# A fifth polynomial tile in every second unit of an attention kernel's first branch

## The chip, the cores and the metric

One core of a Trainium2 chip runs the whole program. The metric is the device time of one execution in microseconds (us).

The five engines work side by side, each through a list of instructions in a fixed order: PE (matrix products; PEld is its weight load), ACT (here nearly only exponentials), DVE and POOL (elementwise work), and SP, which issues most transfers. An instruction that must wait for another engine holds up everything behind it in its own list.

## The reference

Two attention blocks, both over 2048 rows of 1024 columns with 32 heads of 32 columns, all in bf16; the outputs stand side by side.

```
# branch A: full softmax attention
qkv = x @ wqkv
p = softmax(q @ k^T * 32**-0.5)          # 2048 x 2048 in each of 32 heads
a = (p @ v) @ wo

# branch B: four segments of 512 rows; causal softmax inside a segment,
# and a linear memory of the segments before
p = softmax(q_s @ k_s^T * 32**-0.5 + mask)
o = g * (phi(q_s) @ M) / (phi(q_s) @ z + 1e-6) + (1 - g) * (p @ v_s)
M += phi(k_s)^T @ v_s;  z += sum(phi(k_s))     # phi(t) = t + 1 if t > 0 else exp(t)
b = o @ wo

out = concatenate([a, b], axis=-1)
```

## The kernel before

**Units, sets and tiles.** Branch A is cut into 64 units (g, c): four heads (group g, 0 to 7) and 256 queries (c, 0 to 7). A unit has 8 sets of 4 tiles, one tile for each head of the group: 128 partitions by 512 columns, that is two blocks of 128 keys against 256 queries. Branch B has 16 units of 5 such sets, two groups of heads of one segment in each; they are spread among the units of A. The first four units of A are cut into parts, and their sets follow the loading of the input.

**The way of a set.** PE makes the scores (`plan_set`, the products of L1208) in four of six PSUM banks, which serve as three slots of two. ACT turns a slot at a time into `P` (`plan_exp`, L1303: 128 x 1024 elements, scale, exp and a conversion to bf16 in one instruction). Then PE multiplies `P` by the values (L1416) and by ones (L1423) for the sums (`round`); DVE and POOL divide and transpose (`turned`, L1530 to L1550). The two other banks, 6 and 7, take these sums and the projections (the products of L847), whose results DVE copies out (L1623). The text `BANKS` gives the bank of each in turn.

**Polynomial tiles.** Some tiles of A skip ACT. Of a marked set, head 0's tile is computed as a parabola that stands for the exponential of a small argument: DVE reads the scores from PSUM, scales and shifts them into `Y` (L1251, `plan_cube`), POOL squares `Y` into `Z` (L1260) and makes `Pc` of it (L1261, `parabola`). ACT's first exp of that set then has 512 columns instead of 1024. `Y` and `Pc` have three buffers each and `Z` two; the same buffers of `Y` and `Z` serve `phi` of branch B (L1922, `job_phi`), which ends in the same two POOL instructions. A path with ACT's exp is there for arguments that are too large, behind a flag; these inputs do not need it.

Which sets are marked follows from

```
CUBIC = {"3": (0, 2, 4), "4": (0, 2, 4, 6), "5": (0, 1, 2, 4, 6)}
WHOLE = {("A", 7, 7): (0, 2, 4), ("A", 7, 6): (0, 2, 4, 6)}
    def cubed(self, unit, part):
        if unit[0] != "A" or part is not None:
            return ()
        if unit in WHOLE:
            return WHOLE[unit]
        n = 8 * unit[1] + unit[2] if unit[1] < 6 else 48 + PAIR.index(unit[1:])
        return CUBIC[POLYS[n]]
```

`POLYS` has a digit for each unit of A, all of them 4. `PAIR` is the order of the last 16 units. With the four cut units (no polynomial tile) and the two of `WHOLE` this makes 58 x 4 + 4 + 3 = 239 tiles.

**The order.** A planner lays the sets along ACT's time (in `plan_set`, a set with a polynomial tile is shorter by 512 columns), spreads the projections between their ready and due times (`plan_jobs`, `level`), and a list scheduler (`Prog.schedule`) makes one list of instructions for each engine from estimated durations. `rearrange` then changes these lists by `MOVES`: texts for PE, ACT, DVE and POOL, in which "a+b" goes on by a places and takes the instruction b places later forward to here. The lists are fixed from then on; semaphores hold each instruction until what it reads is there.

Of the kernel before, what the change touches and what calls it, by code (L numbers as in the profile page):

```python
# [25 lines left out]
    "666767676767666767766766676667666766676666676666766676666676767767666667666667676767676666766666766676766776766676666766"  # L26
    "667676677676667666667666766676676666667676677676666676666676667666776766776766676666676667666676766776766667666666767667"
    "767666766666766667666766676666666667677676767666667666766676766676767667676667666666676676677676666676666766666667766776"
    "766667666667666766667666667667667666766767767666677666666667676776766666767666667677676766676666667676776766676667666766"
    "67666676666666676666766"  # L30
# [13 lines left out]
POLYS = "4444444444444444444444444444444444444444444444444444444444444444"  # L44
# [101 lines left out]
class Op:  # L146
# [17 lines left out]
    def __hash__(self):  # L164
# [650 lines left out]
class _Kernel:  # L815
# [339 lines left out]
    def cubed(self, unit, part):  # L1155
# [5 lines left out]
        n = 8 * unit[1] + unit[2] if unit[1] < 6 else 48 + PAIR.index(unit[1:])  # L1161
        return CUBIC[POLYS[n]]

# [1132 lines left out]
```

## Time and profile before

| | |
|---|---|
| median of 3 runs | 1057.99 us (1056.72 to 1060.06) |
| profiled execution | 1057.04 us, of which 1055.3 us from its first to its last instruction (the span) |
| busy: PE, ACT, POOL, DVE | 1025.1, 1001.6, 725.4, 708.0 us |
| TensorE clock granted | 1.000 |
| exps of 1024 and of 512 columns | 939 and 239 |
| polynomial tiles | 239 |

Busy is the time in which at least one instruction of the engine runs. The ends of matrix products are modelled by the profiler, so a busy PE is not a PE at its peak. The chain of work that ended last is followed back from the last instruction: at each step to what released it, or to the instruction before it on its engine. A wait is put down to the releaser that came last. The lines of these views stand in the prediction.

### The profile page before, as it was taken

The page shows a single profiled execution, that of the slowest core. Times are in us where ns is not written, and L with a number is a line of the kernel's source. Part 1 is how long each engine was busy: PE and PEld are TensorE (multiplying, and loading weights), DVE is VectorE, ACT ScalarE, POOL GpSimd, SP SyncE. Part 2 cuts the span into 40 slices and gives each one's busy share as a digit, 9 for nine tenths or more (in the row PEclk, how much of TensorE's full clock was granted, in tenths as well). Part 3 has the DMA queues.
Part 4 walks back from the last instruction along what each step waited for, and adds up shares of the span by engine and source line. Part 5 has one row for each costly group of instructions (what it writes and reads, how often), then busy time and mean ns, then how long its engine had stood idle before and what let it go on. Part 6 is the DMA issues. An engine that isn't in the chain of part 4 may idle for free.

```text
span 1055.3 us, 55116 instructions
## 1 busy us (share of the span) xinstructions
PE 1025.1 (97%) x25168; PEld 549.9 (52%) x25168; DVE 708.0 (67%) x1451; ACT 1001.6 (95%) x1193; POOL 725.4 (69%) x999
## 2 busy tenths in 40 slices
PE   8999999999999999999999999999999999999998
PEld 4456555566454455556544454466555545445444
DVE  3446667766656878787647888877556787774444
ACT  4999999999999999999999999999999799999996
POOL 1004677766767888889857897988657688885643
PEclk9999999999999999999999999999999999999999
DMA  9223351007202431034321322033121750022101
GB/s 182 41 43 92 69 140 24 18 14 151 66 28 80 118 85 19 5 59 101 94 73 41 84 57 47 17 86 81 34 77 43 212 147 4 28 78 78 33 23 58
DMA packets 171802, 71.99 MB, mean 68 GB/s; under 512 B 135472, under 2 KB 169776, under 8 KB 171568
## 3 DMA queue, kind: packets, MB, share of 16 engines
q1 hardware_dynamic: 169200, 67.67, 26.7%
q8 instruction: 198, 3.24, 1.3%
q10 hardware_dynamic: 2368, 0.79, 0.3%
q14 instruction: 36, 0.29, 0.1%
HBM read 45.23 MB, written 11.67 MB: 54 GB/s over the span
## 4 chain that ended last, share of the span: by engine, by line
PE 66%; ACT 24%; DVE 5%; POOL 2%; issue 1%; SPq 1%; DMA 0%; ACTq 0%; DVEq 0%; POOLq 0%
PE ps L847 32%; ACT P L1303 24%; PE ps L1208 13%; PE ps L1416 10%; PE ps L1423 9%; DVE Y L1251 1%; DVE T L1530 1%; SPq L1587 1%; POOL Z L1260 1%; PE ps L1877 1%; PE ps L1653 1%; ACT P L1281 1%; DMA xT_A<-in_A_x_dram 0%; DVE OT_B L1959 0%; DVE KQ_B L1623 0%
## 5 line engine op out<-in xcount | busy, mean ns | idle before, releaser
L1303 ACT ACTIVATE P<-ps 128x1024 bf16<-128x1024 f32 (+1 forms) x1178 | 991.9, 988 | 31.7 <-PE ps L1208 16.8
L1260 POOL TENSOR_TENSOR Z<-Y 128x512 f32<-128x512 f32 x287 | 305.6, 1068 | 206.3 <-DVE Y L1251 179.1
L1423 PE MATMUL ps<-P,onesb 128*32 128x256 bf16 (+1 forms) x4386 | 301.0, 270 | 0.0
L1416 PE MATMUL ps<-P,V_A 128*32 128x256 bf16 x3618 | 257.2, 274 | 0.1
L1251 DVE TENSOR_SCALAR Y<-ps 128x512 f32<-128x512 f32 x239 | 163.6, 685 | 113.8 <-PE ps L1208 101.1
L1208 PE MATMUL ps<-KQ_A 32*128 32x256 bf16 x4096 | 203.8, 272 | 10.5 <-ACT P L1303 5.4
L1261 POOL TENSOR_SCALAR Pc<-Z 128x512 bf16<-128x512 f32 x239 | 154.5, 650 | 12.0
L1208 PEld LDWEIGHTS ps<-KQ_A 32*128 32x128 bf16 x4096 | 62.5, 92 | 165.9 <-ACT P L1303 113.0
L1423 PEld LDWEIGHTS ps<-P,onesb 128*32 128x32 bf16 x4386 | 128.6, 96 | 31.4 <-issue 16.0
L847 PE MATMUL ps<-xT_B,W_B 128*32 128x512 bf16 (+1 forms) x2200 | 140.7, 366 | 1.3 <-issue 0.2
L847 PE MATMUL ps<-xT_A,W_A 128*32 128x512 bf16 (+1 forms) x2156 | 140.1, 370 | 1.8 <-DMA xT_A<-in_A_x_dram 1.2
L1416 PEld LDWEIGHTS ps<-P,V_A 128*32 128x32 bf16 x3618 | 107.7, 96 | 34.1 <-issue 15.7
L1416 PE MATMUL ps<-Pc,V_A 128*32 128x256 bf16 x478 | 122.2, 273 | 0.0
L1423 PE MATMUL ps<-Pc,onesb 128*32 128x256 bf16 x478 | 122.1, 273 | 0.0
L1332 POOL TENSOR_SCALAR_AFFINE_SELECT P<-P 128x768 bf16<-128x768 bf16 (+1 forms) x96 | 76.1, 802 | 36.3 <-ACT P L1303 35.4
L1530 DVE STREAM_TRANSPOSE T<-ps 128x512 f32<-128x512 f32 x122 | 86.5, 709 | 16.9 <-PE ps L1423 12.5
L847 PEld LDWEIGHTS ps<-xT_B,W_B 128*32 128x32 bf16 x2200 | 52.8, 96 | 47.2 <-issue 21.8
L847 PEld LDWEIGHTS ps<-xT_A,W_A 128*32 128x32 bf16 x2156 | 50.7, 96 | 46.0 <-issue 13.0
L847 PE MATMUL ps<-Wo_B,OT_B 128*32 128x512 bf16 (+1 forms) x1052 | 70.9, 375 | 0.1
L847 PE MATMUL ps<-Wv_B,xT_B 128*32 128x512 bf16 (+1 forms) x1064 | 69.2, 373 | 0.5 <-DVE T L1441 0.4
L1548 POOL TENSOR_TENSOR T<-T,rc 128x256 bf16<-128x256 f32 x74 | 49.1, 664 | 23.1 <-DVE rc L1533 21.7
L1623 DVE CAST outsb<-ps 128x512 bf16<-128x512 f32 x56 | 38.7, 691 | 37.2 <-PE ps L1416 14.8
(107 smaller groups left out, 1197.7 us busy)
## 6 DMA issues: line engine op xcount, KB each, us to landing
Wv_B<-in_B_wv_dram SPq DMA_DIRECT2D x32, 256.0 KB, 3.4
W_B<-in_B_wk_dram SPq DMA_DIRECT2D x32, 256.0 KB, 3.3
W_B<-in_B_wq_dram SPq DMA_DIRECT2D x32, 256.0 KB, 4.3
Wo_B<-in_B_wo_dram SPq DMA_DIRECT2D x32, 256.0 KB, 3.6
out_dram<-outsb SPq DMA_DIRECT2D x56, 128.0 KB, 1.9
W_A<-in_A_wqkv_dram SPq DMA_DIRECT2D x14, 256.0 KB, 3.9
ot_a_scratch<-OTst SPq DMA_DIRECT2D x50, 64.0 KB, 1.9
xT_A<-ot_a_scratch SPq DMA_DIRECT2D x6, 512.0 KB, 4.9
```

The lines of the kernel that those rows point to most:

```text
L847: ins = e.matmul(out[r], w[:, r], x, start=start, stop=stop, tile_position=(0, 32 * t), skip_group_check=True)
L1208: ins = e.matmul(out, kap, qap, start=st, stop=True, tile_position=(32 * h, 0), skip_group_check=True)
L1251: o = self.dve(lambda e: e.tensor_scalar(Y[:, :], src, SCALE, MID, ALU.mult, ALU.add), 512, key - 9.0, [self.bank[bank]], [rY], fixed=0.15)
L1260: self.pool(lambda e: e.tensor_tensor(Z[:, :], Y[:, :], Y[:, :], ALU.mult), 512, key, [rY], [rZ], rate=0.58)
L1261: return self.pool(lambda e: e.tensor_scalar(dst, Z[:, :], C2, REST, ALU.mult, ALU.add), 512, key, [rZ], [rP], rate=TS_RATE)
L1303: a = self.act(guarded if early and not free else lambda e: e.activation(dst, src, ACT.Exp, scale=SCALE), cols, key, rd, wr, fixed=EXP_FIXED)
L1332: self.pool(lambda e: e.affine_select(v, v, pattern=pat, compare_op=ALU.is_ge, fill=0.0, base=0, channel_multiplier=-1), 2 * nd * P, key + ...
L1416: ins = e.matmul(self.ps[32 * h:32 * h + 32, 512 * obk + q0:512 * obk + q0 + nq], v, p, start=first, stop=last, tile_position=(0, 32 * h), ...
L1423: ins = e.matmul(self.ps[32 * h:32 * h + 32, lcol + q0:lcol + q0 + nq], self.onesb[:, 0:32], p, start=False, stop=last, tile_position=(0, ...
L1530: self.dve(lambda e: e.transpose(T2[:, :], src), 512, k - NORM_K, [obk.res], [ro, rl], fixed=0.17)
L1548: self.pool(lambda e: e.tensor_tensor(half.rearrange("p (b r) -> p b r", r=32), ov, bc, ALU.mult), QC, k, [ro, rr], [rl], rate=0.435)
L1623: self.dve(lambda e: e.tensor_copy(dst, src), 512, key, [self.at(b)], rdst, fixed=0.155)
```

## The change

Every second digit of `POLYS` becomes 5, so that these units take a polynomial tile in set 1 too. The planner's lists and the turns of the banks come out differently, so `BANKS` is new, and so are the texts of `MOVES` for PE, ACT, DVE and POOL: 2933 moves instead of 3463 for PE, 30 instead of 50 for ACT, 1229 instead of 1213 for DVE, 772 instead of 836 for POOL, found by a search that began at the planner's own order. No other line differs.

```diff
 BANKS = (
-    "666767676767666767766766676667666766676666676666766676666676767767666667666667676767676666766666766676766776766676666766"
...
+    "666767667767666767766766676667666766676666676666766676666676767676676667666667676677676666766666766676766776766667666766"
...
 )
...
-POLYS = "4444444444444444444444444444444444444444444444444444444444444444"
+POLYS = "4545454545454545454545454545454545454545454545454545454545454545"
 CUBIC = {"3": (0, 2, 4), "4": (0, 2, 4, 6), "5": (0, 1, 2, 4, 6)}
...
 MOVES = {
     "PE": (
-        "39+1 3+1 1+3 3+1 1+2 1+3 1+1 1+1 1+1 2+1 1+1 1+1 1+1 1+1 1+1 1+1 1+1 1+1 1+1 1+1 1+1 1+1 1+1 1+1 1+1 1+1 1+1 1+1 1+7 7+1 "
...
```

More of the change, by code (lines that the diff above doesn't have):

```diff
@@ L25 @@
 BANKS = (
-    "666767676767666767766766676667666766676666676666766676666676767767666667666667676767676666766666766676766776766676666766"
[L27 to L30, printed above, removed]
+    "666767667767666767766766676667666766676666676666766676666676767676676667666667676677676666766666766676766776766667666766"
+    "667676677676667666667666766676666666667676677676666676666676666667676766776766676676676666666676766776766677666666767667"
+    "767666676666766667666766677666666767667676767667667666766666666676767667676677666666676676677676666676666766666667766776"
+    "766667666667666766667666667667666666766767767677667666666677676776766766766666667677676766676666667676776766676667666766"
+    "67666766666666676666767"
 )
@@ L202 @@
     "PE": (
[123 rows of a table removed]
[103 rows of a table added]
     ),
     "ACT": (
-        "6+1 11+1 1+1 1+1 1+1 1+1 1+1 15+1 1+1 1+1 1+1 1+1 1+1 1+1 1+1 1+1 1+1 1+1 1+1 1+1 1+1 1+1 52+1 1+1 1+1 1+1 1+1 1+1 1+1 "
-        "1+1 1+1 1+1 1+1 1+1 1+1 1+1 1+1 1+1 1+1 1+1 1+1 1+1 1+1 1+1 1+1 1+1 1+1 1+1 1+1 1+1 "
+        "6+1 11+1 1+1 1+1 1+1 1+1 1+1 1+1 14+1 1+1 1+1 1+1 1+1 1+1 1+1 1+1 1+1 1+1 1+1 56+1 1+1 1+1 1+1 1+1 1+1 1+1 1+1 1+1 1+1 "
+        "1081+1 "
     ),
     "DVE": (
[41 rows of a table removed]
[42 rows of a table added]
     ),
     "POOL": (
[28 rows of a table removed]
[26 rows of a table added]
     ),
```

362 rows, old and new, of the table MOVES are left out of this document.

## The prediction

> **What bounds the kernel now.** I read the profile's page first, its chain above all, then the groups by line and shape, then busy time in stretches of 25 us, then the waits, and last the chain inside one stretch.
>
> ```profile
> span 1055.3 us, 55116 instructions
> ...
> PE 1025.1 (97%) x25168; PEld 549.9 (52%) x25168; DVE 708.0 (67%) x1451; ACT 1001.6 (95%) x1193; POOL 725.4 (69%) x999
> ...
> PE 66%; ACT 24%; DVE 5%; POOL 2%; issue 1%; SPq 1%; DMA 0%; ACTq 0%; DVEq 0%; POOLq 0%
> PE ps L847 32%; ACT P L1303 24%; PE ps L1208 13%; PE ps L1416 10%; PE ps L1423 9%; DVE Y L1251 1%; DVE T L1530 1%; SPq L1587 1%; POOL Z L1260 1%; PE ps L1877 1%; PE ps L1653 1%; ACT P L1281 1%; DMA xT_A<-in_A_x_dram 0%; DVE OT_B L1959 0%; DVE KQ_B L1623 0%
> ```
>
> Two engines are nearly full: PE has 30.2 us without work, ACT 53.7 us. The chain says which of them an edit has to shorten: two thirds of the span it runs over PE, a quarter over the exps of L1303. So a microsecond taken from ACT is, on average over the span, worth about a quarter of one. POOL holds 2% of the chain.
>
> The two limits alternate. In the next view the columns are the stretch, its length, and the busy time (with instruction counts) of PE, PEld, DVE, ACT and POOL; the second fence is the same view for the masking of branch B's diagonal tiles (L1332) alone, which shows where units of B lie.
>
> ```profile
> 325.00:350.00 25.00, 25.00 (x596) 12.51 (x588) 17.63 (x29) 24.53 (x31) 20.36 (x24) 1.00 0.19 49
> ...
> 575.00:600.00 25.00, 23.21 (x603) 11.66 (x595) 22.84 (x50) 24.89 (x31) 19.43 (x28) 1.00 0.25 67
> 600.00:625.00 25.00, 25.00 (x620) 13.07 (x612) 19.20 (x36) 23.48 (x29) 23.77 (x33) 1.00 0.32 70
> 625.00:650.00 25.00, 23.09 (x568) 11.75 (x560) 23.01 (x52) 22.92 (x28) 19.01 (x27) 1.00 0.17 40
> 650.00:675.00 25.00, 24.77 (x620) 12.90 (x614) 18.95 (x38) 22.33 (x27) 23.39 (x34) 1.00 0.11 25
> ...
> 925.00:950.00 25.00, 24.21 (x570) 11.89 (x562) 18.64 (x36) 24.25 (x29) 20.60 (x32) 1.00 0.24 77
> ...
> sum 1050.00, PE 1024.40 PEld 549.78 DVE 706.69 ACT 1000.97 POOL 725.43; mean PE 24.39 PEld 13.09 DVE 16.83 ACT 23.83 POOL 17.27
> ```
>
> ```profile
> 575.00:600.00 25.00, 4.87 (x6) 1.00 0.25 67
> 600.00:625.00 25.00, 0.00 (x0) 1.00 0.32 70
> ```
>
> At 575 us, with units of B, ACT is full and PE has 1.8 us to spare. At 600 and 650 us, with units of A alone, PE is full and ACT already idles 1.5 and 2.7 us. The polynomial tiles exist in units of A only: the change relieves ACT mainly where PE is the limit. And in the same stretches POOL, which has 31% to spare over the span, has 1.2 and 1.6 us left of 25.
>
> **The change: what moves.** Of the 32 entries that become 5, four do nothing. The first four units of branch A are cut into parts and take no polynomial tile (this drops the entries of units (0,1) and (0,3)), and (7,6) and (7,7) have their own sets in WHOLE. So 28 units gain one tile each, set 1.
>
> ```profile
> L1303 ACT ACTIVATE P<-ps 128x1024 bf16<-128x1024 f32 x939 | 910.7, 1076 | 26.5 <-PE ps L1208 12.0 <-PE ps L1423 9.7 <-DVE Y L1922 1.3
> L1260 POOL TENSOR_TENSOR Z<-Y 128x512 f32<-128x512 f32 x287 | 305.6, 1068 | 206.3 <-DVE Y L1251 179.1 <-DVE bias L1729 5.3 <-DVE bias L1725 3.8
> ...
> L1251 DVE TENSOR_SCALAR Y<-ps 128x512 f32<-128x512 f32 x239 | 163.6, 685 | 113.8 <-PE ps L1208 101.1 <-POOL Z L1260 3.8 <-PE ps L1423 2.3
> L1261 POOL TENSOR_SCALAR Pc<-Z 128x512 bf16<-128x512 f32 x239 | 154.5, 650 | 12.0
> L1303 ACT ACTIVATE P<-ps 128x512 bf16<-128x512 f32 x239 | 154.3, 645 | 5.2 <-PE ps L1208 4.8
> ```
>
> *ACT.* 28 exps go from 1024 to 512 columns. By busy time one saves 910.7/939 - 154.3/239 = 0.970 - 0.645 = 0.325 us; by mean duration 1076 - 645 = 0.431 us. Halving the columns should halve what scales with them, so I take 0.43: 28 x 0.43 = 12.0 us, and 9.1 us as the low end. ACT's count stays at 1193; its busy time goes to about 990. Of the 12.0 us the chain's share is 24%: -2.9 us. The ends: nothing, if every relieved exp lies where PE leads, and -12.0, if the projections of L847 can be pushed into the stretches where PE has room.
>
> *PE.* The matmuls are the same. 56 pairs of groups (28 tiles, two halves, values and sums) read Pc instead of P; no time.
>
> *DVE.* 28 x 0.685 = 19.2 us more, 708 to 727 us, 69% of the span: free as work. But the tile's PSUM bank is now released by DVE, and the next score matmuls on PE wait for that.
>
> ```profile
> PEld ps L1208 <- ACT P L1303: 133.9, 382, 1.0
> ...
> PEld ps L1208 <- issue: 31.9, 122, 0.8
> ...
> ACT P L1303 <- PE ps L1208: 16.8, 34, 3.2
> ...
> PEld ps L1208 <- DVE Y L1251: 16.3, 45, 0.5
> ...
> DVE Y L1251 <- POOL Z L1260: 3.8, 6, 1.0
> ```
>
> Columns: total us, times, longest. Score matmuls that waited for nothing shown ("issue") still have 31.9/122 = 0.26 us before them; with Y as the releaser it is 16.3/45 = 0.36. The excess is 0.10 x 45 = 4.5 us over 239 tiles, 0.5 us over 28; if all 16.3 counts, 1.9 us. I take 1.0, between the two.
>
> *POOL.* 28 x (1.068 + 0.650) = 48.1 us more, 725 to 774 us, 73%. The same view for PEld alone has PE's waits for it:
>
> ```profile
> PEld ps L1416 <- POOL Pc L1261: 0.6, 3, 0.3
> ```
>
> So POOL has been late rarely: PE waited for Pc three times, DVE for a Y buffer (the row above) six times of 287. What happens when it is late shows in one place. This is the chain in the window 870 to 925 us (start, duration, what):
>
> ```profile
> 911.28 0.36 PE ps L1208 x8
> 911.66 0.70 DVE Y L1251
> 912.43 1.05 POOL Z L1260
> 913.56 0.63 POOL Pc L1261
> 914.26 1.10 POOL Z L1260
> 915.45 0.70 DVE Y L1251
> 916.22 1.05 POOL Z L1260
> 917.35 0.63 POOL Pc L1261
> 918.05 1.05 POOL Z L1260
> 919.20 0.69 DVE Y L1251
> 920.04 0.42 PE ps L1208 x8
> 920.48 5.20 ACT P L1303 x6
> ```
>
> The three Y buffers were full, so DVE could not write the next Y at 914 us; it waited for POOL to square an older one, the PSUM bank stayed taken, and the score matmuls and then the exps stood behind it. Some eight microseconds (911.66 to 920.04) went at POOL's pace. Set 1 makes this likelier: tiles come from sets 0, 1 and 2, three in a row, where today every second set brings one. Over 512 sets of A (64 units of 8) and 80 of B, ACT's 1001.6 us make 1.69 us for a set; POOL needs 1.72 us for its two instructions of a tile and has the outputs' products and the masking of B besides. Three in a row fill the Y and Pc rings (3 each) at once, and the Z ring has 2.
>
> Where POOL has half its time free, this is absorbed. Sixteen of the 38 full stretches from 100 us on have POOL at 20 us or more (first and last quoted above, at 325 and 925); the 28 units lie evenly, so 28 x 16/38 = 12 extra tiles fall there. Each costs nothing or 1.72 us of the chain: 0 to 20.6 us. The groups of POOL in the window 870 to 925 us give how many squarings it held:
>
> ```profile
> L1260 POOL TENSOR_TENSOR Z<-Y 128x512 f32<-128x512 f32 x17 | 18.0, 1057 | 4.4 <-DVE Y L1251 3.8
> ```
>
> Four of these 17 stand in the stretch of chain shown, and two more in the rest of that window's chain:
>
> ```profile
> 875.96 1.05 POOL Z L1260
> ...
> 877.78 1.09 POOL Z L1260
> ```
>
> That is 6 of 17, 35%. By the row of waits it is 6 of 287, 2%. I take a third, because the twelve are in windows as full as this one and get the three in a row on top: 12 x 1.72 / 3 = +6.9 us.
>
> *One rule of the skill.* The squares of L1636 on DVE read two operands from SBUF, and their durations spread far:
>
> ```profile
> L1636 DVE TENSOR_TENSOR sqA<-KQ_A x64: 374/424/1260, 11.1 to 831.3; 128x512 bf16<-128x512 bf16 x64
> ```
>
> These 64, and 64 like them for B, meet POOL's added 48.1 us, 4.6% of the span; at 1.260 - 0.374 = 0.89 us a meeting this is 128 x 0.046 x 0.89 = 5.2 us more on DVE, which at 69% has room, so nothing in the sum. The Trainium skill, "SBUF — State Buffer", section "Who interferes with whom", says that such a DVE instruction and a GpSimd one that reads SBUF exclude each other for the whole instruction; the spread agrees, and by that rule the upper end of DVE's part would be 5.2 us higher.
>
> *The order.* BANKS changes, and the lists of moves are new for PE, ACT, DVE and POOL. No row prices an order that has not run. Bounds: if the waits of PE for exps (133.9 us) grow by an eighth, +16 us; if ACT's 16.8 us of waiting for scores shrink by a third, -5.6. I take 0 and keep both for the range. SP's queue keeps its instructions.
>
> **Sum.** -2.9 + 1.0 + 6.9 = +5.0 us. The profiled execution took 1057.04 us (1.7 us around its span), the median of the runs is 1057.99, 0.95 above it; the difference is applied to the median: 1063.0 us. A change of 0.3%, 3.2 us, is about what a measurement of this kernel can tell from none.
>
> **Rivals.**
> *ACT's time is given back (faster).* The chain runs over exps for 24% of the span, and PE has 1.8 us to spare in windows such as 575. If the projections move into those, half to all of the 12.0 us return: -6 to -12, 1046 to 1052 us. For it: ACT is the engine with the most fixed work outside PE. Against: the relieved stretches are those where PE is at 25.00. Chance 0.29.
> *ACT only idles more (no change).* PE leads in A, POOL's lateness hides behind the order of PE, which holds the polynomial tiles' products back: 1055 to 1061 us, 1058 the middle. For it: 0.6 us of PE waits for Pc. Chance 0.25.
> *The forecast, POOL late three in a row (slower).* It decides from the point where POOL's other work in a unit exceeds what is left beside five tiles, about 4.9 us in a unit of 13.5 (8 x 1.69 less 5 x 1.72). Own range 1061.2 to 1070 us. Chance 0.38.
> *The new order is worse as a whole.* +16 us, 1074 us, with PE waits for exps up everywhere, POOL full or not. Chance 0.08.
>
> **How the numbers follow.** Faster by over 0.3%: 0.29. Within: 0.25. Slower: 0.38 + 0.08 = 0.46. The range goes from 1047, near full use of ACT's saving, to 1073, near the bad order; outside are about 0.05 below and 0.06 above, and what I cannot name. Cases of both signs hold most of the chance; the likeliest one's own range stands above.
>
> **What would show it.** ACT busy near 990 us, with 267 exps of 512 columns and 911 of 1024; POOL near 774 us; 267 Pc. Right: more waits of DVE Y for POOL Z than 6, and POOL's share of the chain above 2%, in stretches where POOL was at 20 us or more. Wrong: PE's idle time falls below 30.2 us with POOL's share unchanged (the first rival), or ACT's idle time rises by about 12 us at the same span (the second). If PE's wait for exps grows where POOL has room, it is the order.

## The result, and the profile after

After takes 1060.91 us (median of 20 runs, 1058.89 to 1065.79), before on the same chip 1058.05 (1056.67 to 1060.13): ratio 1.0034, 95% interval 1.0026 to 1.0041, slower by about 3 us. The forecast was 1063.0. Its sign and size held. Its main reason did not: the added work on POOL shows no cost here, and what costs is the new order, which the sum had entered as 0.

Lines of after are numbered 21 lower: L1303 is now L1282, L1208 L1187, L1251 L1230, L1260 L1239, L1261 L1240, L1416 L1395, L847 L826. The page of after: span, busy times, chain.

```profile
span 1060.2 us, 55229 instructions
...
PE 1024.3 (97%) x25136; PEld 551.8 (52%) x25136; DVE 724.1 (68%) x1479; ACT 994.1 (94%) x1193; POOL 772.5 (73%) x1055
...
PE 66%; ACT 22%; DVE 6%; POOL 2%; issue 1%; SPq 1%; DMA 1%; ACTq 0%; DVEq 0%; POOLq 0%
```

POOL has its 47 us more and DVE its 16, and POOL's share of the chain is what it was, 2%. ACT is busy 7.5 us less, but its idle time went from 53.7 to 66.1 us and the span up by 4.9; PE idles 35.9 us instead of 30.2. The groups of after by shape:

```profile
L1282 ACT ACTIVATE P<-ps 128x1024 bf16<-128x1024 f32 x911 | 887.8, 1069 | 33.7 <-PE ps L1187 17.2 <-PE ps L1402 9.5 <-DVE Y L1901 2.1
L1239 POOL TENSOR_TENSOR Z<-Y 128x512 f32<-128x512 f32 x315 | 335.8, 1069 | 183.5 <-DVE Y L1230 155.4 <-DVE rc L1512 5.3 <-DVE bias L1704 3.7
...
L1240 POOL TENSOR_SCALAR Pc<-Z 128x512 bf16<-128x512 f32 x267 | 174.4, 658 | 16.1 <-PE ps L1402 1.8 <-PE ps L1395 1.4 <-PE ps L826 1.1
L1282 ACT ACTIVATE P<-ps 128x512 bf16<-128x512 f32 x267 | 169.6, 635 | 12.2 <-PE ps L1187 8.8 <-PE ps L1402 2.6
```

All counts are as announced. What is new is the idle time ahead of the exps, and that PE's scores end it. The waits of after (total us, times, longest):

```profile
PEld ps L1187 <- ACT P L1282: 123.2, 346, 1.2
...
PEld ps L1187 <- issue: 35.6, 135, 0.6
...
ACT P L1282 <- PE ps L1187: 26.0, 48, 1.7
...
PEld ps L1187 <- DVE Y L1230: 16.3, 45, 0.6
...
DVE Y L1230 <- POOL Z L1239: 2.2, 3, 1.0
PEld ps L1395 <- POOL Pc L1240: 2.1, 8, 0.4
```

DVE waited for a Y buffer three times, before six times; PE's waits for Pc grew by 1.5 us in all. So POOL is hardly later than before. ACT waits more for scores (16.8 before, 26.0 now), and PE less for exps (133.9, now 123.2): the balance has tipped from ACT to PE.

The picture of the three full Y buffers is not gone: after's chain has it once (start, duration, what).

```profile
261.00 0.70 DVE Y L1230
...
261.77 1.05 POOL Z L1239
...
263.72 1.05 POOL Z L1239
264.79 0.70 DVE Y L1230
...
267.62 1.05 POOL Z L1239
...
268.76 0.69 DVE Y L1230
```

These 8.5 us are as long as the prediction's stretch at 911 us in before. `a_none`, in which the 28 added tiles are 8 columns wide, has the same stretch at 262 us, so the added load is not what makes it.

Where in the span? Both kernels run the same 1184 exps in the same order, so the end of the n-th exp, counted from 0, shows where one falls behind the other (us; the column of before is absolute, the others are differences to it; the last four are experiments told below):

| exp | before | after | a_none | mid | out | ends |
|---|---|---|---|---|---|---|
| 224 | 213.1 | -1.5 | -0.4 | 0.0 | -1.7 | -0.8 |
| 448 | 402.8 | +0.2 | +3.2 | +1.1 | +0.6 | +1.6 |
| 512 | 459.1 | -0.8 | +2.5 | +0.1 | +0.6 | +1.7 |
| 560 | 501.7 | +3.6 | +6.9 | +6.8 | +1.8 | +2.6 |
| 816 | 725.1 | +8.1 | +12.3 | +10.0 | +2.2 | +3.2 |
| 896 | 793.5 | +6.0 | +10.8 | +7.6 | +1.8 | +2.9 |
| 1168 | 1031.7 | +5.2 | +11.6 | +7.9 | +2.7 | +3.6 |

After is level up to exp 512 and falls back by 8.9 us between 512 and 816. Not all of that is time lost. These are the busy times between the two exps (columns as in the prediction), before and then after:

```profile
459.13:725.06 265.93, 257.84 (x6696) 142.90 (x6686) 201.28 (x406) 255.15 (x305) 221.53 (x302) 1.00 0.29 66
```

```profile
458.32:733.15 274.83, 262.51 (x6836) 148.47 (x6832) 211.47 (x422) 253.90 (x305) 237.25 (x321) 1.00 0.29 66
```

PE has 4.7 us more to do there: 1.7 that before does ahead of exp 512, and 3.0 that before does behind exp 816. This is work moved, not time lost. The loss is in PE's idle time, 4.2 us more (12.3 instead of 8.1), since its work over the whole span is the same within 0.8 us. Up to the end of an exp that idle time adds up to (us):

| exp | before | after | a_none |
|---|---|---|---|
| 448 | 9.7 | 10.2 | 13.3 |
| 512 | 11.1 | 12.0 | 15.7 |
| 816 | 19.2 | 24.3 | 28.3 |
| 1168 | 25.2 | 31.2 | 36.9 |

Of the 6.0 us that after loses by exp 1168, 4.2 fall between 512 and 816; `a_none` loses some in every stretch.

The steepest part of the first table is exps 512 to 560. There the busy times are, before and then after:

```profile
459.10:501.70 42.60, 41.11 (x1237) 26.89 (x1232) 33.50 (x72) 41.03 (x50) 39.20 (x56) 1.00 0.50 102
```

```profile
458.30:505.20 46.90, 43.90 (x1312) 29.03 (x1308) 38.06 (x77) 41.00 (x50) 41.89 (x60) 1.00 0.46 93
```

ACT does the same 41.0 us of work. After's list places 75 more matmuls in it, PE has 2.8 us more to do and idles 1.5 us more, and the stretch is 4.3 us longer. Its chain by line, before and then after:

```profile
by line: ACT P L1303 44.9%; PE ps L847 26.9%; PE ps L1208 11.2%; PE ps L1416 8.6%; PE ps L1423 7.3%; DVE T L1530 1.7%; issue 1.3%; PE ps L1708 0.1%
```

```profile
by line: PE ps L826 43.0%; PE ps L1395 14.0%; PE ps L1187 12.9%; PE ps L1402 11.8%; DVE T L1509 5.7%; DVE Y L1230 3.0%; DVE V_A L1602 2.7%; DVE PKQ_B L1915 2.2%; issue 1.6%; DVE T L1420 1.5%; DVE KQ_A L1602 1.5%; DVE OT_B L1938 1.4%; DVEq L
```

In before's list exps are the largest item of this chain; in after's they are not on it, the projections lead with 43%, and POOL does not appear.

### The profile page after: what moved, and what is told of

Read it like the earlier page. It is cut to its first block, busy times and chain, and to the rows that moved or that the text cites. A ratio compares the mean times of both kernels' runs of the same rounds, so it can differ in the third digit from the quotient of the medians.

```text
span 1060.2 us, 55229 instructions
## 1 busy us (share of the span) xinstructions
PE 1024.3 (97%) x25136; PEld 551.8 (52%) x25136; DVE 724.1 (68%) x1479; ACT 994.1 (94%) x1193; POOL 772.5 (73%) x1055
## 4 chain that ended last, share of the span: by engine, by line
PE 66%; ACT 22%; DVE 6%; POOL 2%; issue 1%; SPq 1%; DMA 1%; ACTq 0%; DVEq 0%; POOLq 0%
PE ps L826 32%; ACT P L1282 22%; PE ps L1187 13%; PE ps L1395 10%; PE ps L1402 9%; PE ps L1856 1%; SPq L1566 1%; DVE Y L1230 1%; POOL Z L1239 1%; DVE T L1509 1%; DVE KQ_B L1602 1%; DVE PKQ_B L1915 1%; DMA xT_A<-in_A_x_dram 0%; PE ps L1632 0%; POOL Pc L1240 0%
## 5 line engine op out<-in xcount | busy, mean ns | idle before, releaser
L1282 ACT ACTIVATE P<-ps 128x1024 bf16<-128x1024 f32 (+1 forms) x1178 | 984.1, 970 | 45.9 <-PE ps L1187 26.0
L1239 POOL TENSOR_TENSOR Z<-Y 128x512 f32<-128x512 f32 x315 | 335.8, 1069 | 183.5 <-DVE Y L1230 155.4
L1230 DVE TENSOR_SCALAR Y<-ps 128x512 f32<-128x512 f32 x267 | 182.8, 685 | 111.9 <-PE ps L1187 101.2
L1395 PE MATMUL ps<-P,V_A 128*32 128x256 bf16 x3562 | 256.7, 274 | 1.0 <-DVE T L1509 0.5
L1187 PE MATMUL ps<-KQ_A 32*128 32x256 bf16 x4096 | 204.4, 272 | 12.2 <-ACT P L1282 7.1
L1240 POOL TENSOR_SCALAR Pc<-Z 128x512 bf16<-128x512 f32 x267 | 174.4, 658 | 16.1 <-PE ps L1402 1.8
L1187 PEld LDWEIGHTS ps<-KQ_A 32*128 32x128 bf16 x4096 | 62.7, 92 | 165.5 <-ACT P L1282 105.8
L1402 PEld LDWEIGHTS ps<-P,onesb 128*32 128x32 bf16 x4330 | 128.6, 96 | 26.8 <-issue 12.4
L826 PE MATMUL ps<-xT_A,W_A 128*32 128x512 bf16 (+1 forms) x2160 | 140.2, 370 | 1.7 <-DMA xT_A<-in_A_x_dram 1.0
L826 PE MATMUL ps<-xT_B,W_B 128*32 128x512 bf16 (+1 forms) x2160 | 139.6, 370 | 1.5 <-DVE cols L1695 0.2
L1395 PE MATMUL ps<-Pc,V_A 128*32 128x256 bf16 x534 | 136.5, 274 | 0.7 <-POOL Pc L1240 0.2
L1402 PE MATMUL ps<-Pc,onesb 128*32 128x256 bf16 x534 | 135.7, 273 | 0.0
L1395 PEld LDWEIGHTS ps<-P,V_A 128*32 128x32 bf16 x3562 | 107.5, 96 | 28.6 <-issue 12.2
L826 PEld LDWEIGHTS ps<-xT_B,W_B 128*32 128x32 bf16 x2160 | 51.5, 96 | 46.1 <-issue 21.4
L826 PEld LDWEIGHTS ps<-xT_A,W_A 128*32 128x32 bf16 x2160 | 50.4, 96 | 45.9 <-issue 14.6
L826 PE MATMUL ps<-Wo_B,OT_B 128*32 128x512 bf16 (+1 forms) x1052 | 71.2, 375 | 0.0
L826 PE MATMUL ps<-Wv_B,xT_B 128*32 128x512 bf16 (+1 forms) x1076 | 69.2, 370 | 0.3 <-DVE rc L1512 0.2
L1395 PEld LDWEIGHTS ps<-Pc,V_A 128*32 128x32 bf16 x534 | 51.3, 96 | 27.7 <-issue 12.7
L1602 DVE CAST KQ_A<-ps 128x512 bf16<-128x512 f32 x60 | 41.3, 689 | 34.7 <-PE ps L826 33.8
```

The lines of the kernel that those rows point to most:

```text
L826: ins = e.matmul(out[r], w[:, r], x, start=start, stop=stop, tile_position=(0, 32 * t), skip_group_check=True)
L1187: ins = e.matmul(out, kap, qap, start=st, stop=True, tile_position=(32 * h, 0), skip_group_check=True)
L1230: o = self.dve(lambda e: e.tensor_scalar(Y[:, :], src, SCALE, MID, ALU.mult, ALU.add), 512, key - 9.0, [self.bank[bank]], [rY], fixed=0.15)
L1239: self.pool(lambda e: e.tensor_tensor(Z[:, :], Y[:, :], Y[:, :], ALU.mult), 512, key, [rY], [rZ], rate=0.58)
L1240: return self.pool(lambda e: e.tensor_scalar(dst, Z[:, :], C2, REST, ALU.mult, ALU.add), 512, key, [rZ], [rP], rate=TS_RATE)
L1282: a = self.act(guarded if early and not free else lambda e: e.activation(dst, src, ACT.Exp, scale=SCALE), cols, key, rd, wr, fixed=EXP_FIXED)
```

## The experiments

**1. Order, relief of ACT and load of POOL, one by one.** Three kernels keep after's lists instruction by instruction. `a_free` cuts the 28 added tiles' instructions to 8 columns, `a_wide` keeps ACT's exp of these sets 1024 wide, `a_none` does both, so that nearly only the order is new (84 instructions of 8 columns stay, and DVE, not ACT, still releases the bank of these tiles). `b_act` has before's lists and relieves ACT in the same 28 sets.

```diff
# a_free (a_none too)
-            src = self.ps[:, 512 * bank:512 * bank + 512]
-            o = self.dve(lambda e: e.tensor_scalar(Y[:, :], src,
+            src = self.ps[:, 512 * bank:512 * bank + ny]          # ny = nz = 8 in set 1, else 512
+            o = self.dve(lambda e: e.tensor_scalar(Y[:, 0:ny], src,
...
# in parabola, called with n = nz
-        self.pool(lambda e: e.tensor_tensor(Z[:, :], Y[:, :], Y[:, :], ALU.mult),
...
-        return self.pool(lambda e: e.tensor_scalar(dst, Z[:, :], C2, REST, ALU.mult, ALU.add),
...
+        self.pool(lambda e: e.tensor_tensor(Z[:, 0:n], Y[:, 0:n], Y[:, 0:n], ALU.mult),
...
+        return self.pool(lambda e: e.tensor_scalar(dst[:, 0:n], Z[:, 0:n], C2, REST, ALU.mult, ALU.add),
...
# a_wide (a_none too)
+            if lo and take[0]["set"][3] == 1:
+                src = self.ps[:, c0:c0 + 512].unsqueeze(1).to_broadcast([P, 2, 512])
+                dst = Pt.rearrange("p b n -> p (b n)").bitcast(dt.uint8).rearrange("p (b n) -> p b n", b=2)
# b_act, on before
+            if slot_first and take[0]["set"][3] == 1 and w == 512 and len(self.cubed5(take[0])) == 5:
+                src, dst = self.ps[:, c0 + 512:c0 + 1024], Pt[:, 1, :]
```

`a_free`: 

> The lists of the changed kernel, instruction for instruction; of the 28 added tiles the three instructions (Y on DVE, Z and Pc on POOL) handle 8 columns instead of 512, so their results are left out and ACT's relief is free. Theory POOL (the prediction's: a late POOL costs 6.9 us): the time falls by 6 to 9 us from 1060.9, to 1052 to 1055. Theory ORDER (the new lists cost, POOL's work lies in gaps): it falls by less than 2 us, to 1059 to 1061. Theory ACT-IDLE (the relief is worth nothing, the cost is DVE and POOL): below 1058.

`a_wide`: 

> The changed kernel's lists, the 28 tiles computed on DVE and POOL as there, but ACT's exp of those sets keeps 1024 columns (it reads the second bank twice and writes one byte a column; what it writes is not the probabilities). This takes ACT's relief away and leaves all else. If the relief is worth the chain's share, 24% of 12.0 us, the time rises by 2.9 us, to 1063.8. If ACT sets the pace of these lists, by up to 12 us, to 1073. If the relief is worth nothing, 1061.

`a_none`: 

> Both edits at once: the changed kernel's lists with neither the relief of ACT nor the load of DVE and POOL (8 columns), so what differs from the kernel before is nearly the order alone. Theory ORDER: slower than before by at least the measured 2.9 us, 1061 to 1070. Theory POOL: at or below 1058, since without the load nothing is late.

`b_act`: 

> The kernel before with its own lists; in the same 28 sets ACT's first exp handles 512 columns instead of 1024, and the tile of head 0 is left out (its products read what the buffer held). ACT is relieved by 28 x 0.43 = 12.0 us and nothing is added. By the chain's share the time falls by 2.9 us, to 1055; if ACT's time is not on the path in units of A, 1058; if all of it returns, 1046.

Measured, as a ratio to before on the same chip (1058.9 us, for after 1058.05):

| lists | ACT | load of the 28 tiles | ratio, 95% interval |
|---|---|---|---|
| after's | 1024 | cut (`a_none`) | 1.0102, 1.0089 to 1.0116 |
| after's | 1024 | whole (`a_wide`) | 1.0085, 1.0071 to 1.0099 |
| after's | 512 | cut (`a_free`) | 1.0053, 1.0037 to 1.0068 |
| after's | 512 | whole (after) | 1.0034, 1.0026 to 1.0041 |
| before's | 512 | none (`b_act`) | 0.9993, 0.9984 to 1.0003 |

`a_none` and `b_act` came within what ORDER and "not on the path" foretold, `a_wide` between its two cases. `a_free` missed them all: no theory had it slower than after. The order, without load and relief, costs 1.02%, 10.8 us. Relieving ACT gives 0.49% and 0.51% back in the new lists (5.3 us) and 0.07% in the old (0.6 us, not told from nothing). The load shows no cost in the new lists: both pairs are slightly faster with it (0.17% and 0.19%), but the intervals of each pair overlap. The cut took 36.6 us of POOL's time and 19.4 of DVE's, not all of it, since 8 columns still cost an instruction. The page of `a_none`:

```profile
span 1066.7 us, 55228 instructions
...
PE 1025.0 (96%) x25135; PEld 551.7 (52%) x25136; DVE 705.4 (66%) x1479; ACT 1003.2 (94%) x1193; POOL 737.4 (69%) x1055
...
PE 56%; ACT 34%; DVE 5%; SPq 1%; issue 1%; DMA 1%; POOL 1%; ACTq 0%; DVEq 0%; POOLq 0%
```

Work on PE and ACT is that of before, within 1.6 us, and the span is 11.4 us longer: time in which the lists make engines wait. ACT is 34% of this chain, before 24%: in the new order more of its time is on the path, which fits that relieving it is worth more there. The page of `b_act`:

```profile
span 1055.6 us, 55115 instructions
...
PE 1023.6 (97%) x25167; PEld 550.2 (52%) x25168; DVE 708.9 (67%) x1451; ACT 993.6 (94%) x1193; POOL 725.2 (69%) x999
```

ACT is busy 8.0 us less and the span has not moved. In before's order hardly any of this time was on the path; the forecast's 2.9 us, 0.9973, lies outside the interval.

**2. The load in the old lists.** Before's lists and `b_act`'s relief; the tile of set 0 is worked out twice in the 28 units: on DVE Y and Y again, on POOL Z, Pc and both again.

```diff
             o.urgent = True
+            if twice:                                   # set 0 of the 28 units
+                o = self.dve(lambda e: e.tensor_scalar(Y[:, :], src, SCALE, MID, ALU.mult, ALU.add), 512, key - 9.0,
+                             [self.bank[bank]], [rY], fixed=0.15)
+                o.urgent = True
+                self.pool(lambda e: e.tensor_tensor(Z[:, :], Y[:, :], Y[:, :], ALU.mult), 512, key - BCK, [rY], [rZ], rate=0.58)
+                self.pool(lambda e: e.tensor_scalar(dst, Z[:, :], C2, REST, ALU.mult, ALU.add), 512, key - BCK, [rZ], [rP], rate=TS_RATE)
             last.append(self.parabola(Y, Z, dst, rY, rZ, rP, key - BCK))
```

> The load and ACT's relief without the new order: the lists of before, in the same 28 units ACT's exp of set 1 takes 512 columns (head 0 is left out there), and set 0's polynomial tile is worked out twice: its Y on DVE and its Z and Pc on POOL are issued a second time right behind the first, with the same operands, so that DVE has 28 x 0.52 us and POOL 28 x 1.72 us more and the reads of Pc wait for the second one. Relief alone in these lists was 0.9993 of before. Theory 1 (the tile's load is hidden wherever it stands; what the change costs is its new order): 0.998 to 1.002, about 1058. Theory 2 (the prediction's POOL term holds in the old order, a third of 12 units x 1.72 us): about 1.006, 1064. Theory 3 (before's lists have no room for 1.72 us more ahead of a read of Pc, and the new order is what makes that room): most of 28 x 1.72 = 48 us comes out, at least 1.02, 1080 and more; the kernel's own plan gives +45 us for it.

Measured: 1114.99 us, ratio 1.0533 (1.0514 to 1.0552). Against `b_act` that is 5.4%, 57 us or 2.0 us for each of the 28 tiles: theory 3. Not all of it is waiting: PE is busy 9.2 us longer than in `b_act` over the same matmuls, with a granted clock of 0.995 (`b_act` 0.999). The page of `b_both` (L1270 is the second Y of a doubled tile, L1273 and L1274 its first Z and Pc; L1266, L1281 and L1282 are all the others):

```profile
span 1110.9 us, 55196 instructions
...
PE 1032.8 (93%) x25167; PEld 551.0 (50%) x25168; DVE 726.8 (65%) x1479; ACT 997.9 (90%) x1193; POOL 772.5 (70%) x1055
...
PE 51%; ACT 21%; DVE 12%; POOL 12%; issue 3%; SPq 1%; DMA 0%; DVEq 0%; POOLq 0%; ACTq 0%
```

POOL is exactly as busy as in after, 772.5 us, and is 12% of the chain instead of 2%. Its waits (L1334 is the exp, L1222 the scores, L1447 the products with the values):

```profile
ACT P L1334 <- PE ps L1222: 63.8, 88, 3.2
...
DVE Y L1266 <- POOL Z L1281: 17.9, 12, 2.9
...
PEld ps L1447 <- POOL Pc L1282: 15.1, 16, 2.0
```

And one doubled tile in its chain (start, duration, what):

```profile
221.01 0.70 DVE Y L1266
221.74 0.70 DVE Y L1270
222.51 1.05 POOL Z L1273
223.63 0.68 POOL Pc L1274
224.39 1.05 POOL Z L1281
225.51 0.63 POOL Pc L1282
226.22 1.05 POOL Z L1281
227.36 0.70 DVE Y L1266
```

This is the picture that the prediction drew for the stretch at 911 us: the Y buffers are full, DVE stands until POOL has squared an older one, and score matmuls and exps stand behind it. (A Y takes 0.70 us here, not the 0.52 of the expectation.) So POOL's busy share alone does not price its work: at the same 772.5 us it is 12% of one chain and 2% of the other. But the two loads are not the same case. After's fifth tile has a place and buffers of its own; here the added work stands in series with the tile of set 0, whose reads wait for both. So 57 us is the price of this place, and what a fifth tile at a place of its own costs in the old lists was not tried.

**3. Which stretch of the new lists costs.** Lists joined from both kernels at exps where no instruction had to be moved for the join.

```diff
# the fifth tile in 12, 16 and 10 units; BANKS and the lists to match
-POLYS = "4545454545454545454545454545454545454545454545454545454545454545"
+POLYS = "4444444444444444444444444545454545454545454545454444444444444444"  # mid: after's from exp 440 to 890
+POLYS = "4444454545454545454545454444444444444444444444444545454545454444"  # out: before's from exp 440 to 890
+POLYS = "4444454545454444444444444444444444444444444444444545454545454444"  # ends: before's from exp 230 to 890
```

`mid`: 

> The change in its middle only: before's lists and banks up to exp 440, after's from there to exp 890, before's again behind; the fifth tile in the 12 units that lie wholly in the middle. Theory 1 (the loss sits in the order of this stretch): after gains on before there from +0.7 to +6.1 us late by the two traces, so +5.4 us, 1.005. Theory 2 (each fifth tile costs the same wherever it is): 12 of 28 of the measured +3.4 per mille, 1.0015. Theory 3 (seams between the lists cost more than what lies between them): slower than 1.01.

`out`: 

> The complement: after's lists up to exp 440, before's to exp 890, after's again behind; the fifth tile in the other 16 units. Theory 1: +0.7 us up to exp 440 and 4.9 - 6.1 = -1.2 us behind exp 890, so -0.5 us, 0.9995. Theory 2: 16 of 28 of +3.4 per mille, 1.002. If the stretches add up, this run's and the run before's distances from before sum to after's +3.4 per mille. Theory 3: slower than 1.01.

`ends`: 

> The parts in which after gained on before in the traces: after's lists up to exp 230 and behind exp 890, before's between; the fifth tile in 10 units. Theory 1: about -2.0 us up to exp 230 and -1.2 us behind exp 890: 0.997, 1055, which would beat both kernels. Theory 2: 10 of 28 of +3.4 per mille, 1.0012. If what a stretch gains in one order is used up by the next (a lead in exps that the next stretch waits away), 0.999 to 1.001.

Measured: `mid` 1064.85 us, 1.0055 (1.0041 to 1.0069); `out` 1059.60, 1.0012 (1.0003 to 1.0021); `ends` 1058.77, 1.0001 (0.9992 to 1.0010); before 1058.58. `mid` came as theory 1 has it (1.005 expected), and with 12 of the 28 tiles it reads slower than after with all of them (1.0034): the middle of the new order costs by itself. It is not the only part that does: `a_none` is 3.2 us late before it, at exp 448. The step of `mid` from exp 512 to 560 is in the table, 6.7 us, over the same 1312 matmuls as in after:

```profile
459.20:508.50 49.30, 44.63 (x1312) 29.10 (x1308) 37.86 (x77) 41.06 (x50) 41.62 (x60) 1.00 0.45 93
```

`out` and `ends` miss: 0.9995 and 0.997 were expected. The two complements sum to +6.7 per mille where after has +3.4: stretches do not add up. The table shows what became of the expected gains. After's lead of 1.5 us at exp 224 is 0.8 in `ends` and gone by 448. After's gain of 0.8 us from exp 896 to 1168 turns into a loss of 0.7 to 0.9 in `out` and `ends`, which arrive there less late. In all three PE has 231.8 to 232.1 us of work left there, in before 233.1; but it idles 5.5 us in after, 7.3 in `out` and 6.8 in `ends`. So the gain was work already done, and in the joined lists waiting uses it up; which wait, these traces do not show. Below 1 us such single differences are not to be trusted: `mid` has before's lists up to exp 440 and reads +1.1 at 448. No joined version beats before.

**4. Can another order do better?** New lists for before's program (`s4a`, `s4b`) and after's (`s5a`, `s5b`), each from a search of its own: 1.4 million trial moves on a replay of the planner's timing, with durations fitted to the traces of both kernels. Only `MOVES` differs.

`s4a`: 

> The kernel before (four tiles), its lists changed by a search of 1.4 million trial moves that starts from its own lists and judges them by durations fitted to the two traces (there, releases by ACT cost next to nothing and a score group 0.29 us) instead of the planner's. Theory ORDER (lists are worth 10 us and more, the tile count little): it falls by a third to all of the 14 us that the fit shows, to 1045 to 1054. If the lists of before are already near what the chip allows: 1056 to 1060.

`s4b`: 

> The same search on the kernel before with another random seed: its distance from the other seed tells how far two orders that look equally good lie apart. Theory ORDER: within 3 us of the other seed, 1045 to 1054.

`s5a`: 

> The changed kernel (five tiles in every second unit), searched in the same way from its own lists. Theory ORDER (the new lists, not the fifth tile, make it slower): it comes out level with the searched four tiles or up to 3 us below, 1043 to 1055. Theory POOL (five tiles overload DVE and POOL whatever the order): at least 3 us above the searched four tiles.

`s5b`: 

> The same search on the changed kernel with another random seed. Theory ORDER: within 3 us of its other seed and level with the searched four tiles. Theory POOL: at least 3 us above the searched four tiles, as its other seed.

Measured: 1094.74 us (1.0326, 1.0305 to 1.0348), 1092.16 (1.0323, 1.0304 to 1.0341), 1093.90 (1.0346, 1.0326 to 1.0367) and 1096.97 (1.0358, 1.0338 to 1.0377). A plain miss of some 40 to 50 us. The page of `s4a`, and of its waits one line (L1223 are the scores):

```profile
PE 1040.7 (95%) x26423; PEld 580.9 (53%) x26424; DVE 720.9 (66%) x1451; ACT 1013.1 (93%) x1193; POOL 730.0 (67%) x999
```

```profile
PEld ps L1223 <- issue: 59.3, 231, 0.9
```

The search tore apart pieces that before's lists keep together (projections run as two matmuls of 256 columns instead of one of 512): 1255 matmuls more, PE busy 15.6 us longer at a granted clock of 0.996, and the pauses ahead of score matmuls that nothing shown explains nearly doubled (231 times, before 122). My timing priced none of it. Two things follow. New lists for the same program, with the matmuls they split, moved the time by 34 us. And five tiles against four, each with lists searched in the same way, differ by 0.2 to 0.35%, much like after against before; the intervals overlap, so neither theory is settled by these runs.

## Why the prediction was right, and where it was not

**Sum.** +5.0 us forecast; 2.9 by the medians, 3.6 by the ratio. By the runs, 3.6 is made of +10.8 for the order, -5.3 for ACT in that order and -1.9 for the load. None of the terms was the forecast's: it came near because they happen to cancel, which is luck.

**ACT, -2.9.** The amount, 12.0 us, was about right, though busy time fell by only 7.5 us, and by 8.0 in `b_act`, below the low end of 9.1 (the last section says why). The lever was wrong: the chain's average share is no price. The saving was worth 0.6 us in before's lists and 5.3 in the new ones, where more of ACT lies on the path.

**DVE releasing the bank, +1.0.** The row reads 16.3 us and 45 times, as before. Nothing was added.

**POOL, +6.9: the step that failed.** "I take a third" priced the added tiles by a chain of the old lists, while the kernel measured has new ones. In after neither sign of it came (three waits for a Y buffer, where more than six were foretold; POOL 2% of the chain, where more was), and with the load cut the kernel is no faster: 1.0053 against 1.0034. `b_both` shows that the mechanism exists and can cost far more (57 us) where the work stands in series with a tile of the old lists. The count of full windows was off by one as well: the stretch from 150 to 175 us has POOL at 21.13, so it is 17 of 38, which would add 0.3 us to the term.

**The order, 0: the other failed step.** +10.8 us lies inside the stated bounds (-5.6 to +16), but the value taken was wrong, and the waits that stood for the bounds went another way: PE's waits for exps did not grow (134.1 us in `a_none`, 133.9 before), and ACT's waits for scores grew instead of shrinking. Here are the rows of `a_none` (L1291 is the exp, L1191 the scores):

```profile
PEld ps L1191 <- ACT P L1291: 134.1, 369, 1.1
...
ACT P L1291 <- PE ps L1191: 24.4, 45, 1.6
```

The second row is 7.6 us above before's, of 9.8 us by which ACT's idle time grew. PE's idle time grew by 11.5 us, spread over the span and over many lines; no single wait is shown to be its cause.

**Rivals.** ACT's time was not given back as the first had it (PE's idle time rose). The second named the rise of ACT's idle time by about 12 us, and 12.4 came, but at a longer span. The fourth, with the smallest chance, named the right cause, at too high a price and by a wait that did not grow.

**The rule of the Trainium skill** ("SBUF — State Buffer", "Who interferes with whom"). The squares on DVE (L1636, now L1615) took 69.9 us before and 72.8 after, 2.9 us more with POOL 47 us busier; the estimate was 5.2 at most. One pair of profiles with durations from 354 to 1274 ns does not carry more than that.

## What to carry to other kernels

When an edit comes with a new static order, the rows of the old order do not price the edit: as much work for POOL cost 57 us at one place in the old lists and showed no cost in the new, and the new lists cost 10.8 us by themselves. So enter the order as a term with its full bounds and ask first which engine the stretches will wait for; align two traces by a sequence that both run (here the exps), and look where the lead changes, with the fuller engine's work and idle time kept apart, since a change of lead can be work done earlier and not time won.

## What the runs showed that was not expected

Halving an exp's columns saved 0.27 to 0.29 us of ACT's busy time where the two mean durations differ by 0.43. Yet 0.43 is the price of the work. In a row of exps the next begins before the last has ended, so what one adds to the busy time depends on what stands ahead of it. In before's trace an exp of 1024 columns adds 1.02 us when ACT was idle just before it, and 0.92 us when it follows another; one of 512 columns adds 0.60 and 0.49. Either way half the columns are 0.43 us less, 12.0 us for 28, as forecast. But with less to do ACT idles more often: 136 exps of after start after idle time (`b_act` 137), 102 of before, and each of these 34 or 35 adds 0.10 us more, 3.5 us in all. That leaves 8.5 us, near the 7.5 and 8.0 measured. Busy time over count, 0.325 us, mixes the two cases and is too low a price for the work.

That the added load in after's lists made the kernel 0.17 to 0.19% faster in both pairs, if it is more than chance, is left open.
